# The last layer's GpSimd work moved to VectorE, and half of its weights prepared over sixteen later units

## The chip, the cores and the metric

The kernel runs on one core of a Trainium2 chip. The metric is the device time of one launch in microseconds (us). The engines are named as in the profile: PE is TensorE (matmuls; PEld is its loading of weights), DVE is VectorE, ACT is ScalarE, POOL is GpSimd, SP is the engine that issues the DMAs. Each takes its instructions in the order in which the program has them and waits on semaphores for the others.

## The reference, cut to what matters

Three layers follow one another: an attention with a sigmoid, a soft mixture of experts, and a feed-forward layer with a cosine. The change touches only the last one:

```python
def _moe2_ref(x, w_in, w_out):      # x 1792 x 768, w_in 768 x 2048, w_out 2048 x 768
    h = x @ w_in
    g = h * np.cos(h)
    return (g @ w_out).astype(np.float32)
```

`w_in` and `w_out` come as float64. The product with `w_in` is short here: the mixture's output is a combination of 32 slots, so that `w_in` is first multiplied with the slots (`m4`), and a token's `h` is one product of its slot weights (`ct4`) with `m4`.

## The kernel before, in words

The last layer has four blocks of 448 tokens (t) and sixteen slabs of 128 rows of `w_out` (f): 64 **units** (t, f), which run in the order of t, then f. For each unit:

- `wave`: one matmul gives h (128 x 448, in PSUM; two buffers), and ACT makes the cosine's argument in turns (L953, `ph`).
- `turns` (ACT, L957) rounds it by adding a large constant, and `frac` (DVE, L965) takes off what was rounded. From unit 16 on DVE does both (L969 and L970), and ACT has no `turns`.
- `sine_of` (ACT, L975), then `product` (DVE, L981): g = h times the cosine. The product also releases h's buffer.
- `halves`: ACT writes g's upper part `gh` (L989), and what is left, `gl` (L990), is subtracted by POOL up to unit 14 and by DVE afterwards.
- `out_unit`: 18 matmuls (L1005), for each of six groups of 128 output columns `wh`*`gh`, `wl`*`gh` and `wh`*`gl`, summed in six PSUM banks over the 16 slabs of a block. At a block's end DVE and ACT copy the banks out (L1012), and SP issues a DMA for each.

In the first block every slab of `w_out` is **narrowed** from float64 as well, once for all blocks: ACT takes the magnitude out of the high words (`wo_abs`, L165), three DVE instructions put the bits together (`wo_steps` and `wo_last`: L168, L169, L172, 128 x 768 each), ACT writes the upper part `wh` (`wo_hi`, L906), and POOL subtracts the lower part `wl` (`wo_lo`, L910). Slab 1's `wo_abs` is on POOL. Each narrowed slab lies in one of three buffers `wf`; its source in one of three slots, which a DMA fills again after L172.

The order is written out by hand: in the loop's iteration u stand, engine by engine, the product of unit u+1, the `wave` of unit u+2, `wh` and `wl` of slab u+1, the halves of unit u+1, the first two steps for slab u+2, `frac` and `sine_of` of unit u+2, the third step for slab u+2, and the 18 matmuls of unit u.

Of the kernel before, what the change touches and what calls it, by code (L numbers as in the profile page):

```python
# [32 lines left out]
# a pair's v: three columns of blocks for each head, and one that the two share  # L33
VW = 7 * D
# slots for half a chunk of weights: from the start on, and after the attention for w_out too
W_SLOTS, A_SLOTS = 15, 3
# so many of the first ones are loaded after the attention as well
LATE = 1
# columns of w_in that become float32 at a time, and how many times a pair of heads
CV = 512  # L40
RATE = 1.15
# how far the attention's second product is behind the first
LAG = 2
# steps of a pair of heads that load half a slot, beside every third and fourth
EXTRA = [(i, 1) for i in range(2, 22)]
# steps between the slots' weights and their use
PAUSES = 5
# microseconds that VectorE has in each of a pair's steps for what nothing waits for
SPARE = 0.4, 0.4, 0.8, 1.0
# the difference of the biases of float64 and float32, 1023 - 127, in the upper eight bits of eleven  # L50
F64_SCALE = 2.0 ** -112
# 2^f for f from -1/2 to 1/2, the powers from the first on
# [7 lines left out]
def fused(ctx: ExitStack, tc: tile.TileContext, qk, vv, phi, w1, w2, w_in, w_out, out):  # L60
# [24 lines left out]
    def own_logits(b):  # L85
        """A batch's, tokens to rows; the last one's where no slots' sums are any more."""
        if b < B - 1:
            return l_all[0:CT, b]
        return s_acc.rearrange("p a f -> p (a f)")[0:CT, DM - P:].rearrange("p (c s) -> p c s", c=NC_T)

    # the weights in the order in which they are used, and where each goes
# [8 lines left out]
    # the work space is filled for the first group of experts, after others that are free sooner  # L100
# [6 lines left out]
    def load_half():  # L107
        """A load of weights in two, that it holds up what the attention needs for less long."""
        if not halves_left:
            halves_left.extend(load_w(2))  # L110
        halves_left.pop(0)()
# [45 lines left out]
    def narrow(a, words, dst, eng=None):  # L157
        """float64 bit patterns (low word, high word) to the float32 of their leading bits."""
        low, high = words[:, :, 0], words[:, :, 1]
        # as a float32, the high word has eight of the eleven bits of the exponent in its own exponent;  # L160
        # less the difference of the biases, what three places to the left are a float32's magnitude is left
# [16 lines left out]
    def exp_weights(pool, b, l):  # L178
        """Softmax over the slots (its maximum is taken off), as [hi, lo, hi, lo] for float32r."""
# [30 lines left out]
    # ------------------------------------------------------------ attention and routing  # L210
    with ExitStack() as at:
        # from the first that is free at the end to the last
# [16 lines left out]
        # ahead of what is needed for longer  # L229
# [5 lines left out]
        def load_qk(i):  # L235
            # the second pair's before the first's are done with, where no tokens lie yet
            pool, tag = (xp, "xtok") if i == 1 else (rawp, "raw")
            raw[i] = pool.tile([P, QK], F32, tag=tag, name=f"raw{i}", bufs=2 if i == 1 else 1)
            # the first pair's in two, that the first half is there sooner
# [9 lines left out]
        def split_v(i):  # L249
            """The last 64 rows of two heads, each in its own block, in two parts for float32r."""  # L250
            for j in range(2):
                js = slice(j * D, (j + 1) * D)
                v = v32[i][js, 6 * D:]
                nc.vector.tensor_copy(vh[js, js], v)
                nc.vector.tensor_sub(vl[js, js], v, vh[js, js].bitcast(F32))

        def split_a(i):
            """The last of a pair's weights in two parts for float32r."""
# [5 lines left out]
        def block(i, k):  # L264
            """Queries of two heads, then keys of two heads."""
# [8 lines left out]
        def cast(i):  # L274
            """Both heads' upper parts where only one of them stays, and what the keys' leave."""
# [7 lines left out]
        def cast_keys(i):  # L283
            """The lower part of each head's keys under its upper one."""
# [4 lines left out]
        def cast_queries(i):  # L289
            """Each head's upper part of the queries twice."""  # L290
# [18 lines left out]
        def scores(i, g):  # L309
            """The keys' two parts with the queries' upper one, then the upper part with the lower."""  # L310
            ps = ps_s.tile([P, 2, 512], F32, tag="sc", name=f"sc{i}_{g}")
            rows = [(slice(0, P), j) for j in range(2)] + [(top, 0), (bottom, 1)]
            # the very first of them head by head, as they come
# [45 lines left out]
        def route(i):  # L359
            """Tokens of one pair of heads to rows; logits once a batch has all its pairs."""  # L360
# [13 lines left out]
            if hp == 2:  # L374
                # ahead of what waits, that there is room for the next pair
# [4 lines left out]
            if hp == HP - 1:  # L380
# [3 lines left out]
                else:  # L384
                    # something that the array has left to do while the maximum is on its way
# [5 lines left out]
        def logits(b, half):  # L391
            """Three pairs of heads side by side, each in its own columns of the array."""
# [8 lines left out]
        def warm_up(n, what=ident):  # L401
            """Products for nothing, that the array's clock is up when something comes."""
# [4 lines left out]
        def finish(b):  # L407
            """What a batch adds to the slots' inputs, as a running softmax over all tokens."""
# [7 lines left out]
            def total():  # L416
                ps = ps_a.tile([P, S], F32, tag="lg", name=f"lt{b}")
                # four times, side by side
# [19 lines left out]
                # less the maximum, and as they are  # L438
# [14 lines left out]
            def exponential(out, x, a, f):  # L453
                """2^(n + f), x times log2(e) in two: the table for the scores' sigmoid stays where it is."""
# [6 lines left out]
                    # n + 127 to where a float32 has its exponent  # L461
# [46 lines left out]
            def sums(ps):  # L508
                """What the slots' weights sum up to, for every chunk of tokens."""
# [31 lines left out]
            def last_parts():  # L541
# [6 lines left out]
                # the half first whose place is the first to be used again  # L548
# [29 lines left out]
        # w_in to float32, a piece for each pair of heads  # L578
# [29 lines left out]
        def in_between(i, time):  # L608
            """What VectorE has to do that nothing waits for at once."""
# [11 lines left out]
        with tc.manual_schedule():  # L621
# [9 lines left out]
            # a float32's least exponent for what is less the maximum  # L631
# [57 lines left out]
    # ------------------------------------------------------------ experts  # L689
# [25 lines left out]
    # columns of w_in side by side, two of so many, from here  # L715
# [10 lines left out]
    # what the second 512 columns of the slots give, where the first ones' are no longer needed  # L726
    so2 = s_acc.rearrange("p a f -> p (a f)")[:, 512:512 + 4 * NS].rearrange("p (c r s) -> p c r s", c=2, r=2)

    with ExitStack() as ex:
# [3 lines left out]
        with tc.manual_schedule():  # L733
# [6 lines left out]
            def w1_group(g):  # L740
# [16 lines left out]
                # the second group's go where it came from  # L757
# [20 lines left out]
            def w2_chunk(g, k, c, between=lambda: None):  # L778
                """One chunk for the first 512 columns, two for the others."""
# [19 lines left out]
            def choose(g, k):  # L799
                """Each expert's own slots out of all that went through it, turned."""  # L800
# [7 lines left out]
            def twice(out, chosen, n):  # L808
                """The slots of n chunks, each two times over."""
# [4 lines left out]
            def keep_warm(n):  # L814
                """Products for nothing, that the array's clock stays up where it waits for weights."""
# [7 lines left out]
            # of the 32 slots of each of four experts their own four  # L823
# [18 lines left out]
            # w_in's quarters for all the slots so far, two side by side, while the last columns come  # L842
# [35 lines left out]
    # ------------------------------------------------------------ the last layer  # L878
# [11 lines left out]
    def wo_abs(f, eng=None):  # L890
        if f < NF:
            wf[f] = stg.tile([P, DM], F32, tag="wf", name=f"wf{f}")
            wo[f] = narrow(wf[f], wo[f], wf[f], eng)
# [14 lines left out]
    def wo_lo(f, cols=slice(0, DM)):  # L908
        if f < NF:
            nc.gpsimd.tensor_sub(wl[:, f, cols], wf[f][:, cols], wh[:, f, cols].bitcast(F32))  # L910
# [5 lines left out]
    def m_parts(m, n):  # L916
        """Upper parts stay in the rows where they are, twice, and the lower parts go to the others."""
# [13 lines left out]
    def m_keep(m):  # L931
        """Out of the way of the results."""
# [197 lines left out]
```

## Time and profile before

| | us |
|---|---|
| three runs, median | 601.89 (601.4 to 602.93) |
| span of the profiled execution | 601.1 |
| PE busy | 544.4 (91%) |
| DVE busy | 410.4 (68%) |
| ACT busy | 291.6 (49%) |
| POOL busy | 140.8 (23%) |

The page gives a span from the first to the last instruction, and no time beside it for the profiled execution; the median of the runs is 0.8 us above this span. Busy shares are means over stages: the last layer begins at about 310 us. PE's matmuls overlap in the records, so that a busy time of 367 ns for one of 0.2 us pace is normal.

### The profile page before, as it was taken

The page shows a single profiled execution, that of the slowest core. Times are in us where ns is not written, and L with a number is a line of the kernel's source. Part 1 is how long each engine was busy: PE and PEld are TensorE (multiplying, and loading weights), DVE is VectorE, ACT ScalarE, POOL GpSimd, SP SyncE. Part 2 cuts the span into 40 slices and gives each one's busy share as a digit, 9 for nine tenths or more (in the row PEclk, how much of TensorE's full clock was granted, in tenths as well). Part 3 has the DMA queues.
Part 4 walks back from the last instruction along what each step waited for, and adds up shares of the span by engine and source line. Part 5 has one row for each costly group of instructions (what it writes and reads, how often), then busy time and mean ns, then how long its engine had stood idle before and what let it go on. Part 6 is the DMA issues. An engine that isn't in the chain of part 4 may idle for free.

```text
span 601.1 us, 8006 instructions
## 1 busy us (share of the span) xinstructions
PE 544.4 (91%) x2943; PEld 327.4 (54%) x2943; DVE 410.4 (68%) x786; ACT 291.6 (49%) x471; POOL 140.8 (23%) x114
## 2 busy tenths in 40 slices
PE   8999898979898999777988777888999999999997
PEld 3332223223232353222246565656999999999996
DVE  5899989798999822410039999997655655565553
ACT  5877656655665731100036666645444544444442
POOL 3444424323343300000017566561000000000000
PEclk8999989889898999997999989999999999999999
DMA  6688786773642499999974343302000200020002
GB/s 198 212 300 295 250 279 220 243 256 121 216 162 89 168 318 384 386 385 375 348 263 158 105 151 113 130 28 92 1 0 1 93 0 1 1 93 0 1 1 93
DMA packets 46247, 98.14 MB, mean 163 GB/s; under 512 B 2944, under 2 KB 17664, under 8 KB 46208
## 3 DMA queue, kind: packets, MB, share of 16 engines
q1 hardware_dynamic: 46208, 97.63, 47.1%
q8 instruction: 23, 0.38, 0.3%
q14 instruction: 16, 0.13, 0.1%
HBM read 92.11 MB, written 5.51 MB: 162 GB/s over the span
## 4 chain that ended last, share of the span: by engine, by line
PE 54%; DVE 33%; DMA 4%; issue 4%; SPq 3%; ACT 1%; DVEq 0%; ACTq 0%
PE o L1005 29%; PE sc L321 7%; PE av L345 6%; DVE wf L169 5%; DVE wi L965 4%; DMA w<-in_w 4%; SPq L142 3%; DVE hi L285 2%; PE h L746 2%; DVE hi L286 2%; DVE wf L172 2%; PE av L350 2%; DVE hi L292 2%; DVE wi L172 2%; PE h L951 2%
## 5 line engine op out<-in xcount | busy, mean ns | idle before, releaser
L1005 PE MATMUL o<-gh,wh 128*128 128x448 f32 x384 | 128.9, 367 | 10.2 <-ACT gh L989 9.0
L1005 PE MATMUL o<-gh,wl 128*128 128x448 f32 x384 | 131.4, 374 | 2.7 <-POOL wl L910 2.6
L1005 PE MATMUL o<-gl,wh 128*128 128x448 f32 x384 | 129.7, 369 | 2.5 <-POOL gl L990 2.4
L332 ACT ACTIVATE a<-sc,bias_s 128x896 f32<-128x896 f32 x96 | 87.7, 914 | 63.5 <-PE sc L321 58.8
L975 ACT ACTIVATE wi<-wi 128x448 f32<-128x448 f32 x64 | 37.0, 578 | 108.3 <-DVE wi L970 76.0
L1005 PEld LDWEIGHTS o<-gh,wh 128*128 128x128 f32 x384 | 71.1, 188 | 19.3 <-ACT gh L989 12.4
L1005 PEld LDWEIGHTS o<-gh,wl 128*128 128x128 f32 x384 | 72.7, 192 | 13.4 <-POOL wl L910 7.8
L1005 PEld LDWEIGHTS o<-gl,wh 128*128 128x128 f32 x384 | 72.0, 190 | 11.4 <-POOL gl L990 7.0
L321 PEld LDWEIGHTS <-hi 64*128 64x128 f16 (+3 forms) x384 | 21.8, 99 | 100.1 <-issue 73.7
L345 PE MATMUL av<-a,v 128*64 128x448 f32 x288 | 74.3, 596 | 0.0
L321 PE MATMUL sc<-hi 128*128 128x448 f16 x192 | 52.3, 381 | 17.0 <-DVE hi L293 15.5
L990 DVE TENSOR_TENSOR gl<-wi,gh 128x448 fp32r<-128x448 f32 x49 | 31.9, 651 | 42.8 <-ACT gh L989 42.8
L981 DVE TENSOR_TENSOR wi<-h,wi 128x448 f32<-128x448 f32 x64 | 39.7, 621 | 29.0 <-ACT wi L975 29.0
L953 ACT ACTIVATE wi<-h 128x448 f32<-128x448 f32 x64 | 34.6, 541 | 21.6 <-PE h L951 21.3
L262 POOL TENSOR_TENSOR ar<-a,ar 128x448 fp32r<-128x448 f32 x23 | 28.4, 1235 | 66.2 <-ACT ar L261 66.2
L910 POOL TENSOR_TENSOR wl<-wf,wh 128x768 fp32r<-128x768 f32 (+2 forms) x17 | 33.3, 1958 | 36.6 <-ACT wh L906 36.6
L280 POOL TENSOR_TENSOR hi<-raw,hi 128x448 f16<-128x448 f32 x23 | 25.9, 1126 | 56.9 <-DVE hi L279 40.4
L989 ACT CAST gh<-wi 128x448 fp32r<-128x448 f32 x64 | 35.8, 560 | 5.6 <-DVE wi L981 5.4
L321 PE MATMUL sc<-lo,hi 64*128 64x448 f16 x192 | 37.2, 381 | 0.3 <-DVE lo L304 0.3
L788 PE MATMUL so<-w,zone 128*32 128x512 f32 (+1 forms) x256 | 27.6, 523 | 8.6 <-DMA w<-in_w 8.6
L970 DVE TENSOR_TENSOR wi<-wi 128x448 f32<-128x448 f32 x48 | 30.0, 625 | 1.7
L169 DVE SCALAR_TENSOR_TENSOR wf<-wo,wf 128x768 uint32<-128x768 uint32 x16 | 29.4, 1836 | 0.5
(176 smaller groups left out, 713.1 us busy)
## 6 DMA issues: line engine op xcount, KB each, us to landing
w<-in_w SPq DMA_DIRECT2D x25, 1024.0 KB, 14.3
w<-in_w SPq DMA_DIRECT2D x44, 512.0 KB, 6.9
wi<-in_w_in SPq DMA_DIRECT2D x24, 512.0 KB, 6.6
wo<-in_w_out SPq DMA_DIRECT2D x16, 768.0 KB, 4.3
raw<-in_qk SPq DMA_DIRECT2D x23, 448.0 KB, 3.3
v<-in_vv SPq DMA_DIRECT2D x24, 224.0 KB, 3.6
out_t<-wi SPq DMA_DIRECT2D x24, 224.0 KB, 2.1
zone<-in_w SPq DMA_DIRECT2D x1, 1024.0 KB, 8.5
```

The source lines that it names most:

```text
L169: lambda: nc.vector.scalar_tensor_tensor(out=t, in0=low, scalar=29, in1=t, op0=ALU.logical_shift_right, op1=ALU.bitwise_or),
L321: nc.tensor.matmul(o, kk, q, start=upper, stop=not upper)
L332: nc.scalar.activation(a, ps, AF.Sigmoid, bias=bias_s, scale=qk_scale)
L345: nc.tensor.matmul(av[i][js, 0:S], v32[i][:, vc:vc + D], a[:, j], start=g == 0, stop=False)
L910: nc.gpsimd.tensor_sub(wl[:, f, cols], wf[f][:, cols], wh[:, f, cols].bitcast(F32))
L953: nc.scalar.activation(ph, h, AF.Copy, bias=0.25, scale=inv2pi)
L970: nc.vector.tensor_sub(ph, tn, ph)
L975: nc.scalar.activation(tn, ph, AF.Sin, scale=-2.0 * math.pi)
L981: nc.vector.tensor_mul(g, hs.pop(u), tn)
L989: nc.scalar.copy(gh, g)
L990: (nc.gpsimd if u < NF - 1 else nc.vector).tensor_sub(gl, g, gh.bitcast(F32))
L1005: nc.tensor.matmul(ps, w[:, f, o * P:(o + 1) * P], g, start=f == 0 and w is wh and g is gh, stop=f == NF - 1 and g is gl,)
```

## The change: what it does

- No work of the last layer is on POOL any more: `wo_abs` of slab 1 goes to ACT, `wl` (L910) and `gl` (L995 in the changed kernel) go to DVE for all units.
- The units' order is changed: slabs 0 to 7 of block 0, all 16 slabs of block 1, slabs 8 to 15 of block 0, and then blocks 2 and 3. Slabs 0 to 7 are narrowed at one slab for each unit as before; slabs 8 to 15 are narrowed during units 7 to 21, one slab for two units: the first two DVE steps in an iteration with odd u, the third step, `wh` and `wl` in the next one. Iteration 21 has all of slab 15.
- Block 0's partial sums are copied out of PSUM after unit 7 and are added to the second half's sums after unit 31 by DVE.
- `frac` is one DVE instruction with `turns` on ACT up to unit 23 (before: up to unit 15).
- From unit 7 on the matmuls go column group by column group (before: from unit 15 on).

```diff
     def wo_lo(f, cols=slice(0, DM)):
         if f < NF:
-            nc.gpsimd.tensor_sub(wl[:, f, cols], wf[f][:, cols], wh[:, f, cols].bitcast(F32))
+            nc.vector.tensor_sub(wl[:, f, cols], wf[f][:, cols], wh[:, f, cols].bitcast(F32))
...
-    units = [(t, f) for t in range(B) for f in range(NF)]
+    HALF = NF // 2
+    units = [(0, f) for f in range(HALF)]
+    units += [(1, f) for f in range(NF)] + [(0, f) for f in range(HALF, NF)]
+    units += [(t, f) for t in range(2, B) for f in range(NF)]
+    early = HALF + NF
...
-        if u < NF:
+        if u < early:
             nc.vector.scalar_tensor_tensor(
...
-        (nc.gpsimd if u < NF - 1 else nc.vector).tensor_sub(gl, g, gh.bitcast(F32))
+        nc.vector.tensor_sub(gl, g, gh.bitcast(F32))
...
+                if ends and f < NF - 1:
+                    part[o] = buf(18 + o)
+                    (nc.vector.tensor_copy if o % 2 else nc.scalar.copy)(part[o], ps)
+                elif ends:
                     res = buf(12 + o)
...
+                    if t == 0:
+                        nc.vector.tensor_add(res, ps, part[o])
...
-        wo_abs(1, nc.gpsimd)
+        wo_abs(1)
...
+        def whole(f):
+
+            if f + 1 < NF:
+                later.append(lambda: wo_abs(f + 1))
+            later.append(lambda: wo_steps(f, 2))
+            later.append(lambda: (wo_last(f), wo_hi(f), wo_lo(f)))
...
-            wo_hi(f - 1)
-            wo_lo(f - 1)
+            if f - 1 < HALF:
+                wo_hi(f - 1)
+                wo_lo(f - 1)
             halves(u + 1)
...
-            wo_steps(f, 2)
-            wo_abs(f + 1)
+            if f < HALF:
+                wo_steps(f, 2)
+                wo_abs(f + 1)
+            elif f > HALF and later:
+                for _ in range(2 if f % 2 else 1):
+                    if later:
+                        later.pop(0)()
             frac(u + 2)
```

How this moves instructions is seen in the programs of the engines. First DVE in the first units, one iteration (u = 4 or so), of the kernel before (L981 is the product, L965 `frac`; `wf` is a slab being narrowed, `wi` the work space):

```order
L981 TENSOR_TENSOR wi<-h_2955,wi 128x448
L168 TENSOR_SCALAR wf_2967<-wf_2967 128x768
L169 SCALAR_TENSOR_TENSOR wf_2967<-wo_2906,wf_2967 128x768
L965 SCALAR_TENSOR_TENSOR wi<-wi 128x448
L172 SCALAR_TENSOR_TENSOR wf_2967<-wo_2906,wf_2967 128x768
```

and of the changed one (L986 is the product, L970 `frac`, L995 `gl`):

```order
L986 TENSOR_TENSOR wi<-h_2917,wi 128x448
L910 TENSOR_TENSOR wl<-wf_2901,wh 128x768
L995 TENSOR_TENSOR gl_2962<-wi,gh_2961 128x448
L168 TENSOR_SCALAR wf_2929<-wf_2929 128x768
L169 SCALAR_TENSOR_TENSOR wf_2929<-wo_2868,wf_2929 128x768
L970 SCALAR_TENSOR_TENSOR wi<-wi 128x448
L172 SCALAR_TENSOR_TENSOR wf_2929<-wo_2868,wf_2929 128x768
```

Two subtractions, which read what ACT has just written, stand between the product and L168. Next, DVE in two iterations of the changed kernel's units 8 to 20, an odd one and the even one behind it (the kernel before has no narrowing in its units from 16 on, and between `frac` and the product there nothing either):

```order
L986 TENSOR_TENSOR wi<-h_3455,wi 128x448
L995 TENSOR_TENSOR gl_3494<-wi,gh_3493 128x448
L168 TENSOR_SCALAR wf_3430<-wf_3430 128x768
L169 SCALAR_TENSOR_TENSOR wf_3430<-wo_3330,wf_3430 128x768
L970 SCALAR_TENSOR_TENSOR wi<-wi 128x448
L986 TENSOR_TENSOR wi<-h_3489,wi 128x448
L995 TENSOR_TENSOR gl_3527<-wi,gh_3526 128x448
L172 SCALAR_TENSOR_TENSOR wf_3430<-wo_3330,wf_3430 128x768
L910 TENSOR_TENSOR wl<-wf_3430,wh 128x768
L970 SCALAR_TENSOR_TENSOR wi<-wi 128x448
```

The narrowing stands behind `gl` and ahead of `frac`; the product follows `frac` at once. Last, ACT in the same stretch (L980 is the sine, L958 `ph`, L962 `turns`, L994 `gh`, L165 `wo_abs`, L906 `wo_hi`):

```order
L980 ACTIVATE wi<-wi 128x448
L958 ACTIVATE wi<-h_3355 128x448
L962 ACTIVATE wi<-wi 128x448
L994 CAST gh_3359<-wi 128x448
L165 ACTIVATE wf_3363<-wo_3263 128x768
L980 ACTIVATE wi<-wi 128x448
L958 ACTIVATE wi<-h_3388 128x448
L962 ACTIVATE wi<-wi 128x448
L994 CAST gh_3392<-wi 128x448
L906 CAST wh<-wf_3296 128x768
```

ACT has a sine, `ph`, `turns` and `gh` for each unit, and one instruction of the narrowing behind `gh`.

## Rows read from the trace of the kernel before

**Rows 1.** The page: the span, and TensorE's granted clock in 40 equal slices of the span (tenths of full speed).

```profile
span 601.1 us, 8006 instructions
...
PEclk8999989889898999997999989999999999999999
```

**Rows 2.** The chain of waits in order of time, around 441 us: start, us, what.

```profile
441.09 3.61 PE o L1005 x18
...
444.91 3.60 PE o L1005 x18
```

**Rows 3.** Busy time of each engine in two stretches: length, then PE, PEld, DVE, ACT, POOL (instructions in brackets), PE's granted clock, share of the DMA engines, GB/s.

```profile
325.00:405.00 80.00, 64.41 (x249) 46.20 (x248) 79.39 (x69) 47.56 (x79) 47.91 (x26) 0.96 0.31 109
...
448.00:596.00 148.00, 148.00 (x739) 138.46 (x738) 85.77 (x158) 63.19 (x121) 0.00 (x0) 1.00 0.06 21
```

**Rows 4.** DVE in order of time: start, us, engine, line, operation, out<-in, shapes, and in brackets the idle time before.

```profile
315.68 1.66 DVE L168 TENSOR_SCALAR wf<-wf 128x768 uint32<-128x768 uint32 x1
317.37 1.78 DVE L169 SCALAR_TENSOR_TENSOR wf<-wo,wf 128x768 uint32<-128x768 uint32 x1
...
325.15 0.61 DVE L965 SCALAR_TENSOR_TENSOR wi<-wi 128x448 f32<-128x448 f32 x1
325.69 0.95 DVE L172 SCALAR_TENSOR_TENSOR wf<-wo,wf 128x768 uint32<-128x768 uint32 x1
326.66 0.62 DVE L981 TENSOR_TENSOR wi<-h,wi 128x448 f32<-128x448 f32 x1
327.20 0.55 DVE L168 TENSOR_SCALAR wf<-wf 128x768 uint32<-128x768 uint32 x1
327.79 2.50 DVE L169 SCALAR_TENSOR_TENSOR wf<-wo,wf 128x768 uint32<-128x768 uint32 x1
330.21 1.56 DVE L965 SCALAR_TENSOR_TENSOR wi<-wi 128x448 f32<-128x448 f32 x1
331.69 0.94 DVE L172 SCALAR_TENSOR_TENSOR wf<-wo,wf 128x768 uint32<-128x768 uint32 x1
332.56 0.61 DVE L981 TENSOR_TENSOR wi<-h,wi 128x448 f32<-128x448 f32 x1
...
333.67 0.96 DVE L169 SCALAR_TENSOR_TENSOR wf<-wo,wf 128x768 uint32<-128x768 uint32 x1
334.55 2.29 DVE L965 SCALAR_TENSOR_TENSOR wi<-wi 128x448 f32<-128x448 f32 x1
```

**Rows 5.** POOL in order of time, with the same columns.

```profile
327.60 1.86 POOL L910 TENSOR_TENSOR wl<-wf,wh 128x768 fp32r<-128x768 f32 x1 [3.19 <-ACT wh L906]
329.43 1.86 POOL L990 TENSOR_TENSOR gl<-wi,gh 128x448 fp32r<-128x448 f32 x1
```

**Rows 6.** ACT in order of time, one iteration of the first block.

```profile
331.80 0.58 ACT L975 ACTIVATE wi<-wi 128x448 f32<-128x448 f32 x1 [2.54 <-DVE wi L965]
332.29 0.53 ACT L953 ACTIVATE wi<-h 128x448 f32<-128x448 f32 x1
332.85 0.58 ACT L957 ACTIVATE wi<-wi 128x448 f32<-128x448 f32 x1
333.33 0.81 ACT L906 CAST wh<-wf 128x768 fp32r<-128x768 f32 x1
334.05 0.56 ACT L989 CAST gh<-wi 128x448 fp32r<-128x448 f32 x1
```

**Rows 7.** DVE in order of time, where the first block ends and POOL has nothing more to do.

```profile
409.97 0.62 DVE L970 TENSOR_TENSOR wi<-wi 128x448 f32<-128x448 f32 x1
411.24 0.62 DVE L981 TENSOR_TENSOR wi<-h,wi 128x448 f32<-128x448 f32 x1 [0.64 <-ACT wi L975]
412.55 0.63 DVE L990 TENSOR_TENSOR gl<-wi,gh 128x448 fp32r<-128x448 f32 x1 [0.69 <-ACT gh L989]
413.09 0.39 DVE L969 TENSOR_SCALAR wi<-wi 128x448 f32<-128x448 f32 x1
```

**Rows 8.** ACT in the same stretch.

```profile
410.63 0.58 ACT L975 ACTIVATE wi<-wi 128x448 f32<-128x448 f32 x1 [2.93 <-DVE wi L970]
411.11 0.53 ACT L953 ACTIVATE wi<-h 128x448 f32<-128x448 f32 x1
411.95 0.57 ACT L989 CAST gh<-wi 128x448 fp32r<-128x448 f32 x1 [0.31 <-DVE wi L981]
```

**Rows 9.** DVE's subtractions of other widths, grouped, from 316 to 405 us: count | busy us, mean ns | idle before.

```profile
L929 DVE TENSOR_TENSOR m<-wi,m 64x512 fp32r<-64x512 f32 x2 | 1.4, 686 | 0.1
L929 DVE TENSOR_TENSOR m<-m,m 64x384 fp32r<-64x384 f32 x2 | 1.1, 555 | 0.1
```

**Rows 10.** PE in order of time, around a longer wait in the first block.

```profile
345.23 0.47 PE L951 MATMUL h<-ct,m 128*128 128x448 f32 x1 [0.41 <-DVE wi L981]
347.19 1.47 PE L1005 MATMUL o<-gh,wh 128*128 128x448 f32 x6 [1.49 <-ACT gh L989]
349.26 2.51 PE L1005 MATMUL o<-gh,wl 128*128 128x448 f32 x6 [0.60 <-POOL wl L910]
```

**Rows 11.** The columns of rows 3, just behind that wait.

```profile
348.40:351.80 3.40, 2.80 (x9) 2.28 (x8) 3.40 (x3) 1.84 (x4) 2.29 (x2) 0.65 0.00 0
```

**Rows 12.** Who waited for whom from 413 to 597 us: us in total, times, longest.

```profile
DVE gl L990 <- ACT gh L989: 42.0, 48, 1.0
...
PE o L1005 <- DVE wi L1012: 0.7, 1, 0.7
```

More of the change, by code (lines that the diff above doesn't have):

```diff
@@ L888, in fused, with wo_abs @@
     wf = {}
-    def wo_abs(f, eng=None):
+    def wo_abs(f):
         if f < NF:
             wf[f] = stg.tile([P, DM], F32, tag="wf", name=f"wf{f}")
-            wo[f] = narrow(wf[f], wo[f], wf[f], eng)
+            wo[f] = narrow(wf[f], wo[f], wf[f])
     def wo_steps(f, n):
@@ L935, in m_keep @@
         m_ps[m] = t
-    units = [(t, f) for t in range(B) for f in range(NF)]
-    gs, acc = {}, {}
+    HALF = NF // 2
[3 more added lines that the diff above has]
+    early = HALF + NF
+    gs, acc, part = {}, {}, {}
     def buf(k):
@@ L996, in out_unit @@
         terms = [(wh, gh), (wl, gh), (wh, gl)]
+        begins = u == 0 or units[u - 1][0] != t
+        ends = u == len(units) - 1 or units[u + 1][0] != t
         if order is None:
-            order = [(range(NO), [k]) for k in range(3)] if u < NF - 1 else [(range(NO), range(3))]
-        for os, part in order:
+            order = [(range(NO), [k]) for k in range(3)] if u < HALF - 1 else [(range(NO), range(3))]
+        for os, ks in order:
             for o in os:
-                if f == 0 and part[0] == 0:
-                    acc[o] = bank(o, f"o{t}_{o}")
+                if begins and ks[0] == 0:
+                    acc[o] = bank(o, f"o{u}_{o}")
                 ps = acc[o][:, 0:S]
-                for w, g in [terms[k] for k in part]:
+                for w, g in [terms[k] for k in ks]:
                     nc.tensor.matmul(
                         ps, w[:, f, o * P:(o + 1) * P], g,
-                        start=f == 0 and w is wh and g is gh, stop=f == NF - 1 and g is gl,
+                        start=begins and w is wh and g is gh, stop=ends and g is gl,
                     )
-                if f == NF - 1:
+                if ends and f < NF - 1:
+                    part[o] = buf(18 + o)
+                    (nc.vector.tensor_copy if o % 2 else nc.scalar.copy)(part[o], ps)
+                elif ends:
                     res = buf(12 + o)
-                    copy = nc.vector.tensor_copy if o % 2 else nc.scalar.copy
-                    copy(res, ps)
+                    if t == 0:
+                        nc.vector.tensor_add(res, ps, part[o])
+                    else:
+                        (nc.vector.tensor_copy if o % 2 else nc.scalar.copy)(res, ps)
                     nc.sync.dma_start(out=out[o * P:(o + 1) * P, t * S:(t + 1) * S], in_=res)
@@ L1065, in fused @@
         out_unit(0, [((4, 5), (0, 2, 1))])
+        later = []
+        def whole(f):
[3 more added lines that the diff above has]
+            later.append(lambda: (wo_last(f), wo_hi(f), wo_lo(f)))
+        for f in range(HALF, NF):
+            whole(f)
         for u in range(1, len(units)):
@@ L1072, in fused @@
             wave(u + 2)
-            if u > 1 and u + 2 < NF:
+            if 1 < u < early - 2:
                 turns(u + 2)
-            wo_hi(f - 1)
-            wo_lo(f - 1)
+            if f - 1 < HALF:
+                wo_hi(f - 1)
+                wo_lo(f - 1)
             halves(u + 1)
@@ L1079, in fused @@
                 turns(u + 2)
-            wo_steps(f, 2)
-            wo_abs(f + 1)
+            if f < HALF:
[5 more added lines that the diff above has]
+                        later.pop(0)()
             frac(u + 2)
-            ends = u % NF == NF - 1
+            ends = u == len(units) - 1 or units[u + 1][0] != units[u][0]
             if not ends:
                 sine_of(u + 2)
-            if f < NF:
+            if f < HALF:
                 wo_last(f)
```

## The prediction

> **What bounds the kernel now.** I read the page first, then the chain of waits, the busy time by stretches, and the engines in order of time around the end of the first block. The page's granted clock shows that TensorE runs at full speed nearly everywhere in the last layer [rows 1]. The chain of waits shows the steady state of blocks 1 to 3: 18 matmuls in 3.61 us and one `wave`, so 3.81 us a unit, with nothing else on the path [rows 2]; in that stretch PE is busy all the time and DVE for 85.77 of 148 us [rows 3]. The change can gain nothing there, since the number of matmuls stays. The stretch before, 325 to 405 us, is the reverse: DVE is busy for 79.39 of 80 us, PE for 64.41 [rows 3]. From one L172 to the next it takes 331.69 - 325.69 = 6.00 us a unit [rows 4]. About 2.2 us a unit over fifteen units are what there is to gain.
>
> The rows of DVE show why it takes 6.00. L169 takes 0.96 us at 333.67 and 2.50 at 327.79; `frac` takes 0.61 at 325.15 and 1.56 or 2.29 later [rows 4]. The long ones lie where POOL has its two subtractions of 1.86 us each [rows 5]. So POOL's work beside DVE costs DVE about 2.5 us a unit.
>
> **The change part by part.** I follow DVE, since it sets the pace, by steps from start to start where no wait lies between: `frac` 0.54, L172 0.87, product 0.54, L168 0.59, L169 0.88 without POOL [rows 4], `gl` 0.54 [rows 7]. `wl` on DVE at 768 columns is not in the trace. Its neighbours are 555 ns at 384 columns and 686 ns at 512 [rows 9], 0.131 us for 128 columns, which gives 0.95 us at 768 (an estimate; a step of 0.87). The bounds are 0.69, as at 512 columns, and 1.26, twice `gl`'s 0.63.
>
> *First units (iterations 2 to 6).* DVE has 0.87 (L172) + 0.54 (product) + 0.87 (`wl`) + 0.54 (`gl`) + 0.59 + 0.88 + 0.54 = 4.83 us of work in an iteration. But `wl` now waits for `wh` on ACT, and ACT comes to it only after the sine, `ph` and `turns`: 333.33 - 331.80 = 1.53 us after the sine's start, and it takes 0.81 [rows 6]. The sine starts 0.04 after `frac` ends [rows 7, 8]. The loop is therefore sine to `wh` 1.53, `wh` 0.81, hand-over 0.03, `wl` 0.87, `gl` 0.54, L168 0.59, L169 0.88, `frac` 0.61, hand-over 0.04 = 5.90 us. DVE waits about 1.1 us in each. So what POOL's absence gives back is spent: 5.90 against 6.00.
>
> *Ahead of them.* L168 and L169 of slab 1 go from 1.66 + 1.78 to 0.55 + 0.96 and L169 of slab 2 from 2.50 to 0.96 [rows 4], 3.5 us less; five subtractions come in (about 1.7 us for slab 0 and unit 0, 1.6 for slab 1 and unit 1), and some waits for ACT. I take -0.3 us, bounds -1.5 and +1.5: L172 of slab 2 starts at 325.4 instead of 325.69. Five loops and 0.5 for the piece of `m4` in iteration 4 bring L172 of slab 7 to 355.4. Iteration 6 has no L168 and L169 any more, so its `frac` ends at 355.4 + 0.07 + 5.90 - 1.47 = 359.9.
>
> *Units 7 to 21.* Here narrowing stands behind `gl` and ahead of `frac`, and nothing stands between `frac` and the next product. So two waits, which the first units cover with L172, lie open: from the end of `frac` to the start of `gl` pass 0.04, the 1.53 that ACT needs for sine, `ph` and `turns`, `gh` 0.56 and 0.03 [rows 6, 8], together 2.16 us, in which DVE does only the product. The same two waits are there in blocks 1 to 3 (0.64 before the product, 0.69 and more before `gl`) [rows 7, 12], but with 1.0 us of `frac` and nothing else in the iteration they end within PE's 3.81. Now:
> - odd iteration: 2.16 + `gl` 0.54 + L168 0.59 + L169 0.88 + `frac` 0.61 = 4.78 us;
> - even iteration: 2.16 + 0.54 + L172 0.95 + 0.03 + `wh` 0.81 + 0.03 + `wl` 0.87 + `frac` 0.61 = 6.00 us, since `wl` stands directly behind `wh`, which waits for L172.
>
> The pair takes 10.78, or 5.39 us a unit against PE's 3.81. PE has no part in it: `wave` of unit u+2 follows the matmuls of unit u-1; these start with `gl` of that unit, made in iteration u-2, and last 3.6 us, while ACT wants the `wave` in iteration u. The DMAs of `w_out` are issued one for two units, each for a slab three slabs ahead, some 30 us. Iteration 7 ends at 359.9 + 4.78 = 364.7. Iteration 8 has three copies of partial sums in front (1.55) that hide the sine's wait and a piece of `m4` inside the wait for `gh`; its `gl` comes 0.7 later than in others: 364.7 + 6.7 = 371.4. Six pairs (9 to 20) end at 371.4 + 64.7 = 436.1. Iteration 21 has all of slab 15: 2.16 + 0.54 + 0.59 + 0.96 + 0.03 + 0.95 + 0.03 + 0.81 + 0.03 + 0.87 + 0.61 = 7.6, so 443.7. Sine, product and `gh` (1.97 with hand-overs) let unit 23's first matmul start at 445.7.
>
> *The sum.* In the kernel before, unit 23 starts at 441.09 [rows 2]: +4.6 us. PE then waits 0.3 for `gl`, and in unit 24 for the copies of block 1's banks, which stand behind two more iterations on DVE: 1.0 (the kernel before has 0.7 once, at its first block end [rows 12], already inside its 441.09). From unit 25 on both kernels have the same 39 units at 3.81 us. Block 0's end at unit 31 has six additions of 0.62 on DVE instead of three copies; each goes along with its column group of 0.6 us, and PE needs the bank a unit later, so 0 (at worst 0.7, as at that block end).
>
> *The clock.* [...] PE waits longest before unit 23, 7.6 - 3.8 = 3.8 us, where it becomes the bound: 0 to 2 us, of which the wait for the copies would absorb 1.0; I take 0.4.
>
> Total: 4.6 + 0.3 + 1.0 + 0.4 = +6.3 us, a span of 607.4, and 608.2 for the median, which stands 0.8 above the span.
>
> [...] In row terms: L969 at 413.09 has had its input since ACT's L953 at 411.11 ended, at 411.64, and DVE was idle for 0.69 from then on, yet it ran after `gl` [rows 7, 8]. [...]
>
> **Rivals.**
> - *Narrowing is hidden behind PE* (faster). For it: DVE's work in units 8 to 22 is 0.54 + 0.54 + 0.54 + (0.59 + 0.88 + 0.87 + 0.87)/2 = 3.2 us a unit, under 3.81. Unit 8 would start at about 363 and unit 25 at 363 + 17 x 3.81 + 1 = 428.8 instead of 441.09 + 7.62 = 448.7: 582. Against it: the work must be done in the program's order, with two round trips to ACT in an odd and three in an even iteration. It would decide if a round trip cost DVE under 0.3 us. Chance 0.08.
> - *DVE does not wait for `wh` in the first units* (no change). 4.83 instead of 5.90 takes 5 x 1.07 = 5.4 us off the forecast: 602.8. For it: L172 is over 0.6 us before the product ends. Against it: ACT's order, with `wh` behind `ph` and `turns`. Chance 0.05.
> - *The clock stays low* (slower still). [...] Chance 0.05.
>
> **How the numbers follow.** The forecast has 0.82. Its own bounds: `wl` at 0.69 or 1.26 instead of 0.95 is thirteen times -0.26 or +0.31, so -3.4 or +4.0; with the prologue and the clock 604 to 612, which is the range. A measurement of this kernel can tell 0.3% (1.8 us) from no change. Faster 0.09 (first rival and a little of the second), same 0.06 (second rival, lower end of the forecast), slower 0.85.
>
> **What would show it.** Right: no POOL in the last layer; L169 always near 0.96; in units 8 to 22 DVE busy for about 60%, waiting on ACT before product, `gl` and `wl`; unit starts on PE alternately 4.8 and 6.0 apart; unit 23 near 446; after unit 25 3.81 again. Wrong: unit starts 3.8 apart from unit 8 on, `wl` far from 0.95, or matmuls 0.4 us apart for whole units.

## The result and the profile after

The changed kernel takes 609.64 us (median of 4 runs, 605.16 to 610.45) against 601.91 (601.4 to 602.93). The ratio over all runs is 1.0115, with an interval of 1.0072 to 1.0158. It is slower: by 7.7 us from median to median, by 6.9 by that ratio; 6.3 were forecast.

The page of the changed kernel, its span, its busy times and the granted clock in 40 slices, where [rows 1] has the kernel before:

```profile
span 603.4 us, 8002 instructions
...
PE 541.2 (90%) x2943; PEld 329.7 (55%) x2943; DVE 396.5 (66%) x816; ACT 296.3 (49%) x480; POOL 79.8 (13%) x81
...
PEclk9999999999898999979997989999989999999999
```

This profiled execution is the one that took 605.16 us, and its span is only 2.3 us above that of before. The layers ahead of the last one, whose instructions are the same, were 5.1 us shorter in it: the last layer's first `wave` starts at 305.82 us instead of 310.94, and from 100 to 150 us the granted clock was 1.00 instead of 0.86. In a second profiled execution (after_again, below), with a span of 608.5, the first `wave` starts at 311.43. So all comparisons below count from the first `wave`. By that count the last layer grew from 286.53 to 294.26 us, 7.7 us, and in the second execution by 7.3.

Where the 7.7 us came from is seen in the starts of the units on PE (first output matmul, us after the first `wave`):

| | unit 8 | unit 16 | unit 22 | unit 23 | unit 24 | unit 25 |
|---|---|---|---|---|---|---|
| before | 53.97 | 102.27 | 126.18 | 129.99 | 133.81 | 137.62 |
| changed | 53.43 | 95.63 | 128.36 | 135.79 | 141.55 | 145.36 |

The changed kernel is 6.6 us ahead at unit 16, where it has four slabs still to narrow and the kernel before none. It has lost that and 5.8 us more by unit 23, and another 1.9 by unit 25. From there on both run at 3.81 us a unit.

The busy times by stretches (columns as in [rows 3]): the first units, units 8 to 20 by DVE's iterations, the stretch around unit 23, and the steady state:

```profile
325.00:354.00 29.00, 22.27 (x101) 18.23 (x99) 23.77 (x35) 17.64 (x30) 0.00 (x0) 1.00 0.37 126
359.64:431.97 72.33, 62.50 (x264) 48.65 (x263) 46.75 (x69) 37.94 (x66) 0.00 (x0) 0.98 0.16 55
441.00:444.40 3.40, 3.26 (x10) 2.37 (x11) 2.13 (x4) 1.57 (x3) 0.00 (x0) 0.75 0.00 0
444.40:447.20 2.80, 2.80 (x12) 2.54 (x11) 2.13 (x6) 1.86 (x4) 0.00 (x0) 0.69 0.22 82
456.00:590.00 134.00, 134.00 (x669) 125.31 (x668) 81.08 (x150) 57.32 (x109) 0.00 (x0) 1.00 0.06 22
```

DVE was full in the first stretch before (79.39 of 80 us, [rows 3]). Now it is busy for 23.77 of 29 us there and for 46.75 of 72.33, 65%, in units 8 to 20, where PE is not full either. No engine is the bound by its busy time; what is, DVE in order of time shows (columns as in [rows 4]):

```profile
331.85 0.95 DVE L172 SCALAR_TENSOR_TENSOR wf<-wo,wf 128x768 uint32<-128x768 uint32 x1
...
334.40 0.96 DVE L910 TENSOR_TENSOR wl<-wf,wh 128x768 fp32r<-128x768 f32 x1 [1.07 <-ACT wh L906]
...
336.39 0.96 DVE L169 SCALAR_TENSOR_TENSOR wf<-wo,wf 128x768 uint32<-128x768 uint32 x1
...
337.81 0.95 DVE L172 SCALAR_TENSOR_TENSOR wf<-wo,wf 128x768 uint32<-128x768 uint32 x1
...
378.12 0.62 DVE L986 TENSOR_TENSOR wi<-h,wi 128x448 f32<-128x448 f32 x1 [0.70 <-ACT wi L980]
379.61 0.63 DVE L995 TENSOR_TENSOR gl<-wi,gh 128x448 fp32r<-128x448 f32 x1 [0.87 <-ACT gh L994]
...
382.94 0.62 DVE L986 TENSOR_TENSOR wi<-h,wi 128x448 f32<-128x448 f32 x1 [0.70 <-ACT wi L980]
384.44 0.63 DVE L995 TENSOR_TENSOR gl<-wi,gh 128x448 fp32r<-128x448 f32 x1 [0.87 <-ACT gh L994]
384.98 0.95 DVE L172 SCALAR_TENSOR_TENSOR wf<-wo,wf 128x768 uint32<-128x768 uint32 x1
386.83 0.96 DVE L910 TENSOR_TENSOR wl<-wf,wh 128x768 fp32r<-128x768 f32 x1 [0.90 <-ACT wh L906]
...
389.03 0.62 DVE L986 TENSOR_TENSOR wi<-h,wi 128x448 f32<-128x448 f32 x1 [0.70 <-ACT wi L980]
```

The upper part is one loop of the first units, L172 to L172 in 337.81 - 331.85 = 5.96 us; L169 takes 0.96, as everywhere in the layer now, and 1.07 us are lost waiting for `wh`. The lower part is an odd and an even iteration: product to product 4.82 and 6.09, 10.91 us the pair, with waits of 0.70 + 0.87 in the one and 0.70 + 0.87 + 0.90 in the other. The chain of waits over the even iteration (start, us, what) shows the work passing between the two engines with no piece of PE in it, where [rows 2] has nothing but PE:

```profile
382.33 0.58 ACT wi L980
382.90 0.44 ACT wi L958
...
383.37 0.58 ACT wi L962
383.95 0.46 ACT gh L994
...
384.44 0.63 DVE gl L995
385.06 0.88 DVE wf L172
...
385.96 0.84 ACT wh L906
...
386.83 0.96 DVE wl L910
387.79 0.55 DVE wi L970
```

Every piece of ACT in it is a time in which DVE stands still or does the product alone.

### The profile page after: what moved, and what is told of

It reads as the page before. It is cut to its first block, busy times and chain, and to the rows that moved or that the text cites. A ratio compares the mean times of both kernels' runs of the same rounds, so it can differ in the third digit from the quotient of the medians.

```text
span 603.4 us, 8002 instructions
## 1 busy us (share of the span) xinstructions
PE 541.2 (90%) x2943; PEld 329.7 (55%) x2943; DVE 396.5 (66%) x816; ACT 296.3 (49%) x480; POOL 79.8 (13%) x81
## 4 chain that ended last, share of the span: by engine, by line
PE 43%; DVE 32%; ACT 10%; DMA 6%; issue 5%; SPq 3%; POOL 0%; DVEq 0%; ACTq 0%; POOLq 0%
PE o L1012 27%; DMA w<-in_w 5%; PE sc L321 4%; PE av L345 3%; DVE hi L285 3%; SPq L142 3%; DVE hi L286 2%; DVE wi L172 2%; DVE wf L169 2%; ACT wi L980 2%; DVE wi L169 2%; DVE wi L970 2%; DVE hi L292 2%; ACT wi L962 2%; ACT wh L906 2%
## 5 line engine op out<-in xcount | busy, mean ns | idle before, releaser
L1012 PE MATMUL o<-gh,wh 128*128 128x448 f32 x384 | 138.8, 376 | 11.8 <-ACT gh L994 9.0
L1012 PE MATMUL o<-gl,wh 128*128 128x448 f32 x384 | 138.0, 373 | 0.0
L1012 PE MATMUL o<-gh,wl 128*128 128x448 f32 x384 | 136.2, 369 | 0.1
L980 ACT ACTIVATE wi<-wi 128x448 f32<-128x448 f32 x64 | 37.0, 578 | 104.2 <-DVE wi L975 62.9
L1012 PEld LDWEIGHTS o<-gh,wh 128*128 128x128 f32 x384 | 73.9, 193 | 22.6 <-ACT gh L994 14.3
L1012 PEld LDWEIGHTS o<-gl,wh 128*128 128x128 f32 x384 | 73.9, 192 | 9.5 <-DVE gl L995 5.1
L995 DVE TENSOR_TENSOR gl<-wi,gh 128x448 fp32r<-128x448 f32 x64 | 40.0, 625 | 46.1 <-ACT gh L994 46.0
L321 PE MATMUL sc<-hi 128*128 128x448 f16 x192 | 50.3, 369 | 17.6 <-DVE hi L293 16.1
L986 DVE TENSOR_TENSOR wi<-h,wi 128x448 f32<-128x448 f32 x64 | 39.9, 623 | 34.5 <-ACT wi L980 34.4
L958 ACT ACTIVATE wi<-h 128x448 f32<-128x448 f32 x64 | 34.4, 538 | 15.7 <-PE h L956 15.4
L994 ACT CAST gh<-wi 128x448 fp32r<-128x448 f32 x64 | 35.7, 558 | 6.0 <-DVE wi L986 5.8
L956 PE MATMUL h<-ct,m 128*128 128x448 f32 x64 | 25.8, 403 | 13.1 <-DVE wi L986 11.5
L975 DVE TENSOR_TENSOR wi<-wi 128x448 f32<-128x448 f32 x40 | 25.0, 625 | 1.4
L281 POOL TENSOR_TENSOR lo<-raw,hi 128x448 f16<-128x448 f32 x23 | 24.9, 1082 | 0.0
```

Of the source, the lines that this page charges most:

```text
L321: nc.tensor.matmul(o, kk, q, start=upper, stop=not upper)
L958: nc.scalar.activation(ph, h, AF.Copy, bias=0.25, scale=inv2pi)
L980: nc.scalar.activation(tn, ph, AF.Sin, scale=-2.0 * math.pi)
L986: nc.vector.tensor_mul(g, hs.pop(u), tn)
L994: nc.scalar.copy(gh, g)
L995: nc.vector.tensor_sub(gl, g, gh.bitcast(F32))
```

## The experiments

Theory A (the prediction's): the pace of units 1 to 22 is a chain of round trips between DVE and ACT, in the program's order; the added narrowing stands behind the waits and not in them. Rival B: the amount of work decides, so that DVE or PE is short of time, or PE's clock. Rival C: the loss comes from the new order itself (copies, additions, DMAs of the slabs) and not from the subtractions on DVE.

**lo_late: `wl` one iteration after `wh`.** One of the three waits in an even iteration goes; the work stays.

```diff
-            later.append(lambda: (wo_last(f), wo_hi(f), wo_lo(f)))
+            later.append(lambda: (wo_last(f), wo_hi(f)))
+            later.append(lambda: wo_lo(f))
...
-                for _ in range(2 if f % 2 else 1):
+                for _ in range(3 if f % 2 and f > HALF + 1 else 2 if f % 2 else 1):
```

> The changed kernel, but in units 8 to 22 the subtraction of wl is moved out of the even iterations to the next odd one, behind gl, so that DVE does not stand waiting for wh; the same work on every engine. 'Round trips' theory (DVE's waits for ACT, in the order of the program, set the pace of these units): the wait of 0.90 us and the step of 0.87 leave the even iteration (6.09 to 4.3), 0.88 comes into the odd one (4.82 to 5.7): the pair takes 10.0 instead of 10.91 us, six pairs and iteration 21 give 6 us, about 604 us. 'Volume' theory (DVE has too much work): no change, 609. 'Clock' theory (PE at the lower clock sets the pace): no change, 609.

Measured: 600.84 us against 601.61 in the same session, ratio 0.9993 (0.9967 to 1.0019); the last layer takes 286.88 us, 7.4 less than in the changed kernel. DVE:

```profile
375.79 0.62 DVE L986 TENSOR_TENSOR wi<-h,wi 128x448 f32<-128x448 f32 x1 [0.70 <-ACT wi L980]
...
382.20 0.95 DVE L910 TENSOR_TENSOR wl<-wf,wh 128x768 fp32r<-128x768 f32 x1
...
385.86 0.62 DVE L986 TENSOR_TENSOR wi<-h,wi 128x448 f32<-128x448 f32 x1 [0.70 <-ACT wi L980]
```

`wl` has no wait any more and the pair takes 385.86 - 375.79 = 10.07, as expected. The time was forecast 3 us too high. By the unit starts, 5.4 us of the gain lie in the six pairs and 0.8 in iteration 21 (unit 22 to 23 takes 6.59 us instead of 7.43), about as expected; another 1.4 lie in iteration 8 (unit 10 starts at 61.52 instead of 62.90), which the expectation had left out. The end of block 1 gives nothing: slab 15's `wl` now comes in iteration 22, and PE waits 1.06 us for it in unit 23.

**steps_late: L168 and L169 behind `frac`.** They move to where DVE waits for the sine.

```diff
-                for _ in range(2 if f % 2 else 1):
-                    if later:
-                        later.pop(0)()
+                if f % 2 == 0:
+                    later.pop(0)()
+                elif len(later) > 2:
+                    later.pop(0)()
             frac(u + 2)
+            if f > HALF and f % 2 and later:
+                later.pop(0)()
+                if len(later) == 1:
+                    later.pop(0)()
```

> The changed kernel, but in the odd iterations of units 7 to 21 the first two steps of narrowing stand behind frac instead of ahead of it, so that they lie in DVE's wait for the sine; the same work on every engine. Round trips: 0.70 us less in every odd iteration (4.82 to 4.1), the pair 10.2 instead of 10.91, about 4.9 us in all, 605 us. Volume or clock: no change, 609.

Measured: 601.40 against 601.61, ratio 1.0007 (0.9986 to 1.0028), the last layer 286.57 us, 7.7 less than changed, where 4.9 were expected. The rows say why (DVE, and in the last line PE ahead of unit 23):

```profile
381.30 0.62 DVE L986 TENSOR_TENSOR wi<-h,wi 128x448 f32<-128x448 f32 x1 [0.70 <-ACT wi L980]
...
385.33 0.62 DVE L986 TENSOR_TENSOR wi<-h,wi 128x448 f32<-128x448 f32 x1
386.58 0.62 DVE L995 TENSOR_TENSOR gl<-wi,gh 128x448 fp32r<-128x448 f32 x1 [0.63 <-ACT gh L994]
...
391.17 0.62 DVE L986 TENSOR_TENSOR wi<-h,wi 128x448 f32<-128x448 f32 x1 [0.70 <-ACT wi L980]
...
438.24 0.47 PE L956 MATMUL h<-ct,m 128*128 128x448 f32 x1 [1.91 <-DVE wi L986]
```

The pair takes 391.17 - 381.30 = 9.87 instead of the 10.2 expected. The product at 385.33 has no wait, and since it comes later, ACT is through `ph` and `turns` by then, so that the wait for `gh` falls too, from 0.87 to 0.63. I had counted one wait where moving the work shortens two, which is 2 us over six pairs. Most of the rest lies at the end of block 1: PE's pause before unit 23 is 1.91 us, the matmuls behind it are 0.20 us apart from the fourth on (439.81, 440.01), and units 23 and 24 take 8.98 us together instead of 9.57.

**cover: the same instructions, put into the waits.** In units 6 to 21 (one iteration earlier than in the changed kernel, so that slab 15 has two as well) one of the four DVE instructions of a slab stands between `gh` and `gl` and one behind `frac`; ACT's two go behind `gh`.

```diff
         nc.scalar.copy(gh, g)
+        between()
         nc.vector.tensor_sub(gl, g, gh.bitcast(F32))
...
+        def slot(u, k):
...
+            if not odd:
+                wo_steps(g, 1)
+            elif k == 0:
+                wo_last(g)
+            else:
+                wo_lo(g)
...
-            halves(u + 1)
+            halves(u + 1, lambda: slot(u, 0))
+            beside(u)
...
             frac(u + 2)
+            slot(u, 1)
```

> The changed kernel with the narrowing of slabs 8 to 15 put into DVE's waits: of a slab's four DVE instructions L168 lies in the wait for gh and L169 in the wait for the sine of one iteration, L172 and wl in those of the next (from iteration 6 on); the same work on every engine. Round trips: DVE's iteration falls to about 3.5 us, PE becomes the bound at 3.81 us a unit from unit 8 on, unit 25 starts 27 us earlier: about 583 us. Volume: no change, 609. Clock: no change or little, over 600.

Measured: 582.93 against 601.61, ratio 0.9683 (0.9621 to 0.9745); the last layer 267.63 us, 26.6 less than changed. Its chain of waits in units 12 and 13:

```profile
380.19 3.60 PE o L1013 x18
...
384.00 3.61 PE o L1013 x18
```

and DVE beside it:

```profile
380.54 0.55 DVE L168 TENSOR_SCALAR wf<-wf 128x768 uint32<-128x768 uint32 x1
381.87 0.63 DVE L996 TENSOR_TENSOR gl<-wi,gh 128x448 fp32r<-128x448 f32 x1 [0.78 <-ACT gh L994]
382.41 0.62 DVE L970 SCALAR_TENSOR_TENSOR wi<-wi 128x448 f32<-128x448 f32 x1
382.95 0.95 DVE L169 SCALAR_TENSOR_TENSOR wf<-wo,wf 128x768 uint32<-128x768 uint32 x1
383.82 0.62 DVE L986 TENSOR_TENSOR wi<-h,wi 128x448 f32<-128x448 f32 x1
```

PE is the bound at 3.81 us a unit from unit 8 on, with the same instructions in another order. This rules out B for units 8 to 22: neither engine had too much work there, and the clock was not what held them up. It also rules out C as far as copies and DMAs go, since they are in this kernel too.

**no_pool: POOL's work moved, the old order of units kept.**

```diff
-    HALF = NF // 2
...
+    HALF = NF
+    units = [(t, f) for t in range(B) for f in range(NF)]
+    early = NF
...
-            if 1 < u < early - 2:
+            if u > 1 and u + 2 < NF:
```

> One part of the change alone: the units in the order of the kernel before, all sixteen slabs narrowed in the first block, but POOL's work (wl, gl, wo_abs of slab 1) on DVE and ACT as in the changed kernel. Round trips: what DVE gains without POOL beside it, it loses in waiting for wh, 5.95 us an iteration instead of 6.00: 601 to 602 us, as before. Volume: DVE has 4.83 us of work in an iteration, fifteen units by 1.1 us less: 585 to 588.

Measured: 598.89 against 601.61, ratio 0.9964 (0.9942 to 0.9985), the last layer 284.05 us, 2.5 less than before. The time is 2 to 3 us below the expectation, though the loop is 5.96, as expected (335.92 to 341.88, product to product). Most of the gain, 1.8 us, lies between units 8 and 16. At the block's end the kernel before has PE waiting for POOL's last `wl` (start, us, idle time in brackets),

```profile
409.21 0.47 PE L1005 MATMUL o<-gh,wl 128*128 128x448 f32 x1 [0.98 <-POOL wl L910]
```

and with `wl` on DVE that wait is gone, which accounts for about half of the 1.8; the rest I did not trace. I had left this end out of the expectation.

**with_pool: the new order of units, `wl` and `gl` left on POOL.** (`gl` up to unit 22.)

```diff
-            nc.vector.tensor_sub(wl[:, f, cols], wf[f][:, cols], wh[:, f, cols].bitcast(F32))
+            nc.gpsimd.tensor_sub(wl[:, f, cols], wf[f][:, cols], wh[:, f, cols].bitcast(F32))
...
-        nc.vector.tensor_sub(gl, g, gh.bitcast(F32))
+        (nc.gpsimd if u < early - 1 else nc.vector).tensor_sub(gl, g, gh.bitcast(F32))
```

> The other part of the change alone: the new order of units, with slabs 8 to 15 narrowed over units 7 to 21, but wl for all slabs and gl up to unit 22 on POOL as in the kernel before. Round trips: DVE has no wl and gl to stand waiting for, so only the wait for the sine is left, though POOL lengthens its instructions again by 2 to 3 us a pair: about 9 us a pair instead of 10.91, 595 to 602 us in all. Volume: POOL takes 1.6 us a unit from DVE, so less as well, down to PE's pace from unit 8 on: about 585. If neither DVE's waits nor its work count: 609.

Measured: 592.69 against 601.0, ratio 0.9848 (0.9806 to 0.989): 1.5% faster than before, and 2.7% faster than with the subtractions on DVE. DVE's groups from 380 to 430 us (count | busy us, mean ns | idle before):

```profile
L168 DVE TENSOR_SCALAR wf<-wf 128x768 uint32<-128x768 uint32 x6 | 10.8, 1797 | 0.0
L169 DVE SCALAR_TENSOR_TENSOR wf<-wo,wf 128x768 uint32<-128x768 uint32 x6 | 10.8, 1792 | 0.2
L986 DVE TENSOR_TENSOR wi<-h,wi 128x448 f32<-128x448 f32 x12 | 7.5, 625 | 10.0 <-ACT wi L980 10.0
```

and POOL in order of time, with one `frac` of DVE ahead of it:

```profile
377.99 0.62 DVE L970 SCALAR_TENSOR_TENSOR wi<-wi 128x448 f32<-128x448 f32 x1
378.06 1.56 POOL L995 TENSOR_TENSOR gl<-wi,gh 128x448 fp32r<-128x448 f32 x1 [3.54 <-ACT gh L994]
379.58 1.86 POOL L910 TENSOR_TENSOR wl<-wf,wh 128x768 fp32r<-128x768 f32 x1
```

L168 and L169 cost 1.80 each, 2.1 us a pair more than without POOL, and still the pair takes 8.34 (product at 379.52 to product at 387.86) instead of 10.91, and of the 9 or so expected: the waits for `gh` and `wh` are now POOL's, which has nothing behind them in a hurry. What is left on DVE is the wait for the sine. So the two halves of the change each gain when they are alone and lose together:

| | old order of units | new order |
|---|---|---|
| `wl`, `gl` on POOL | 601 to 602 us | 592.7 |
| `wl`, `gl` on DVE | 598.9 | 609 |

So C is out as well: the new order costs nothing by itself, and gains with POOL.

**cover_all: cover, and L168 and L169 of the first units between `wh` and `wl`.**

```diff
                 wo_hi(f - 1)
+                if f < HALF:
+                    wo_steps(f, 2)
                 wo_lo(f - 1)
...
             if f < HALF:
-                wo_steps(f, 2)
                 wo_abs(f + 1)
```

> The kernel that puts the narrowing of slabs 8 to 15 into DVE's waits, and in iterations 1 to 5 as well: there L168 and L169 of the next slab stand ahead of wl instead of behind gl, so that DVE does not stand waiting for wh; the same work on every engine. Round trips: DVE's iteration falls from 5.96 to its 4.83 us of work in five iterations, 5 to 6 us below the 582.9 of the run without this: about 577.5 us. Volume: no change against that run, 583. Clock: no change, 583.

Measured: 578.16 against 601.0, ratio 0.9611 (0.9584 to 0.9639), the fastest of all; the last layer 263.15 us. Its stretches (columns as above):

```profile
325.00:354.00 29.00, 25.41 (x115) 21.82 (x113) 27.68 (x42) 21.65 (x37) 0.00 (x0) 0.96 0.48 161
366.00:432.00 66.00, 66.00 (x330) 61.73 (x330) 53.25 (x87) 44.78 (x80) 0.00 (x0) 1.00 0.19 69
```

In the first units DVE's loop takes 4.81 us (L172 at 329.50 and 334.31) instead of 5.96 and DVE is busy for 27.68 of 29 us instead of 23.77, and in the second stretch PE is busy all the time, with DVE at 53.25 of 66. The wait of 1.07 us for `wh` was worth 4.5 us on top of cover (267.63 - 263.15).

**no_pool_cover: the same edit of the first units, with the old order of units** (all sixteen slabs at one a unit).

> The units in the order of the kernel before and no work on POOL, and L168 and L169 of the next slab ahead of wl in all iterations of the first block. Round trips: 4.83 instead of 5.96 us in some twelve iterations, 13 us below the 598.9 of the run without this: about 586 us. Volume: no change, 599.

Measured: 584.55 against 601.0, ratio 0.9731 (0.9703 to 0.9759), the last layer 270.19 us, 13.9 less than no_pool. So the new order of units, with its waits covered, is worth another 7.0 us of the layer (270.19 - 263.15).

**fill: twelve matmuls with zero weights in PE's longest pause**, after unit 22. They add zero to a bank that is summed anyway. The question is whether the slow unit 23 comes from the pause: then it is shorter with the fill, and otherwise it stays as long.

```diff
+        zero = gp.tile([P, P], F32R, tag="zero", name="zero", bufs=1)
+        nc.scalar.activation(zero, ident, AF.Copy, scale=0.0)
...
+            if u == 22:
+                for _ in range(12):
+                    nc.tensor.matmul(acc[5][:, 0:S], zero, gs[u][0], start=False, stop=False)
```

> The changed kernel with twelve matmuls with a weight of zeros behind unit 22's, which add nothing to the sums and fill PE's wait before unit 23. [...]

Around unit 23 PE in the changed kernel reads (the same columns as [rows 10]):

```profile
441.02 0.47 PE L956 MATMUL h<-ct,m 128*128 128x448 f32 x1 [2.69 <-DVE wi L986]
...
443.58 0.57 PE L1012 MATMUL o<-gh,wh 128*128 128x448 f32 x1
443.96 0.57 PE L1012 MATMUL o<-gh,wl 128*128 128x448 f32 x1
...
446.17 0.37 PE L1012 MATMUL o<-gh,wl 128*128 128x448 f32 x1
```

and with the fill:

```profile
442.12 2.60 PE L1123 MATMUL o<-gh,zero 128*128 128x448 f32 x12
444.99 0.47 PE L956 MATMUL h<-ct,m 128*128 128x448 f32 x1 [0.27 <-DVE wi L986]
...
451.23 0.47 PE L1012 MATMUL o<-gh,wh 128*128 128x448 f32 x1 [0.70 <-DVE wi L1024]
```

After the pause of 2.69 us the matmuls come up to 0.38 apart (443.58 to 443.96), against 0.20 in the steady state, and the granted clock is 0.75 from 441.00 to 444.40 and 0.69 from there to 447.20; unit 23 took 5.76 us from its start to that of unit 24. With the fill it takes 4.18, its matmuls 0.20 apart from the fourth on (446.55, 446.76), which fits the pause as the cause, though in one execution only. steps_late points the same way without a fill: a shorter pause of 1.91 us, matmuls 0.20 apart, and 4.17 us for unit 23. But now PE has to wait 0.70 for the copies of block 1's banks, which the slow unit 23 had hidden, and unit 24 takes 4.79 us instead of 3.81. Unit 25 starts at 144.97 after the first `wave`: 0.4 earlier than the 145.36 above, but not earlier than in after_again, which has 144.90 without a fill. So no gain of the fill is shown. One run took 608.5 us, which the spread of the changed kernel's runs does not tell from no effect.

**after_again: the changed kernel once more**, to see its layer in an execution whose layers ahead are not shorter.

> The changed kernel, unchanged, once more, for its last layer and its time beside the kernel before on another chip. If the loss is in the last layer, its length from the first wave to the last copy is again 7 to 8 us above the 286.5 of the kernel before, whatever the layers ahead of it take, and the time is 1.0 to 1.4% above. If the loss of the first comparison came from the spread of the earlier layers, the last layer's length varies as well.

Measured: 608.97 (607.69 to 610.33, 6 runs) against 601.36, ratio 1.0119 (1.0084 to 1.0155), with the layer at 293.83 us.

## Why the prediction was right

The forecast was 608.2 us; 609.64 and 608.97 were measured, and the mechanism was that of the forecast. Step by step:

- *`wl` on DVE.* Estimated 0.95 from two narrower subtractions [rows 9]; measured 0.96. The line through 384 and 512 columns holds at 768.
- *First units.* Forecast 5.90 a loop, measured 5.91 and 5.96; the wait for `wh` 1.07, forecast "about 1.1". The second rival (no wait there) is out. L172 of slab 2 starts 14.83 us after the first `wave`, where the forecast gives 325.4 - 310.94 = 14.5: the prologue gained nothing (14.75 before) instead of 0.3. The first loop took 5.29, which made up for it by luck, and L172 of slab 7 starts at 44.42, forecast 44.5.
- *Units 7 to 21.* The term of 10.78 for the pair was 0.13 too small: 10.91. From `frac`'s end to `gl`'s start pass 2.20 instead of 2.16, twice a pair, and `wh` takes 0.84 in the chain instead of 0.81. Six pairs make 0.8 us of it. Iteration 21 took 7.67, forecast 7.6.
- *Unit 23.* Forecast +4.6, measured +5.8. Of the 1.2 the pairs are 0.8 and iterations 8 and 21 some 0.3; the rest is that the forecast took the unit's start of before from the chain, 441.09, where PE's own record has 440.93.
- *The end of block 1.* Forecast 0.3 for `gl`, 1.0 for the copies and 0.4 for the clock, 1.7 together; measured 1.9. The sum came out nearly right by luck, since two of its parts were mis-sized. Where the matmuls of unit 23 are 0.20 apart from the fourth on (fill, steps_late), it takes 4.18 and unit 24 4.79 us (fill), so that `gl` costs about 0.4 and the copies 1.0, as forecast. In the changed kernel the lower clock (granted 0.75 and 0.69) costs 5.76 - 4.18 = 1.6 us, and 1.1 in after_again, and the copies are hidden behind it: unit 24 takes 3.81. That they would overlap stood in the prediction as a possibility, and the size of the clock's term (0.4, of 0 to 2 us) was taken too low: no run shows the 0.4, which was the author's estimate, and in its place the runs showed these 1.6 and 1.1 us in the changed kernel, with unit 23 at 4.18 and 4.17 in fill and steps_late. With the 1.2 above, this makes the 7.7 of the layer instead of 6.3.
- *The clock in units 8 to 22.* A lower clock was rare there, and hidden: of the even units only unit 14 had one (granted 0.72 from 390 to 396 us; in after_again unit 18 has matmuls 0.37 apart). It took 5.76 us and the next one 5.16, 10.92 the pair like the others.
- *Unit 31's additions.* Forecast 0: the units from 25 on run at 3.81 in both kernels.
- *From span to time.* The profiled run's time stands 1.8 us above its span (605.16 and 603.4), not 0.8, which came from comparing before's median with one execution. It matters little, since the forecast in effect added 6.3 to the 601.9 of before.
- *The program's order.* DVE kept to it here, as at L969 before the change [rows 7, 8]: the same instructions in two program orders take 294.26 and 267.63 us; in the changed one DVE stands still for 0.87 ahead of `gl` with L168 queued behind it, which in cover runs in just that place.
- *The first rival* (narrowing hidden behind PE, 582 us) was priced rightly and rejected rightly for this kernel: cover, in which the waits are filled by the program's order, takes 582.93. *The third* (clock low throughout) is out: the granted clock was 0.98 from 359.64 to 431.97.

## What to carry to other kernels

Adding up each engine's busy time per unit says how fast a stretch could be; how fast it is, the round trips in each engine's own order say: here DVE was busy for 65% of units 8 to 20 and set their pace of 10.91 us a pair. When an edit moves work to an engine that waits for another one, write down its instructions in order with the waits between them, and look for what could stand in each wait: here that order alone was worth 26.6 to 31.1 us. And two edits that gain alone can lose together, because each may use up the slack in which the other was hidden; they have to be measured as a square of four kernels, not one after the other.

## What the runs showed of the hardware beyond that

Beside POOL, L168, with one tensor and a constant, goes from 0.55 to 1.80 us in with_pool, and L169, with two tensors, from 0.96 to 1.79. Not each overlap does it: `frac` at 377.99 in with_pool takes 0.62 although POOL's `gl` runs from 378.06 on, where before the change it took 1.56 beside the same instruction [rows 4, 5]. The order of the starts goes with it. In the last layer of the kernel before, all 9 L169 that start while a subtraction of POOL runs take 1.78 to 2.59 us, and all 6 that start ahead of one and overlap it take 0.96; of `frac`, the 13 that start while one runs take 1.56 to 2.29, and the one that starts first takes 0.62. In with_pool from 378 to 402 us the three L168 and the three L169 that start while a subtraction runs take 1.79, and the three `frac` that start first take 0.62.

PE's pauses in units 8 to 22 cost nothing: the pair with the lower clock, units 14 and 15, took 10.92 us, like the others. The pause of 2.69 us before unit 23, where PE becomes the bound again, was followed by a lower clock (0.75 and 0.69) that cost about 1.6 us; before the change a wait of 1.49 had been followed by a granted clock of 0.65 [rows 10, 11]. The length of the pause alone does not decide: the 1.91 us in steps_late were followed by matmuls 0.20 apart, and of the changed kernel's five pauses of 1.11 us ahead of even units only the one before unit 14 was followed by a lower clock (0.72; 1.00 behind the other four). What does decide stays open. In the changed kernel's units 8 to 25 a pause had a price only where PE's own pace counted behind it, before unit 23, and there it hid the wait for the copies, which is 0.70 us in fill.
